# A planner's allowance for transfers: two microseconds on every landing, and queries loaded right behind keys and values

## The chip, the cores and the metric

The kernel runs on one core of one Trainium2 chip. The metric is the device time of one execution in microseconds (us); of the kernel before there are 8 timed executions, and one further look with the hardware profiler.

## The reference, cut to what matters

Linear attention with cosine weights feeds a two-layer network with squared ReLU. Eight batches (B), eight heads (H), 576 positions (S), head width 64 (D); the network goes from 512 to 2048 and back.

```python
def phi(x, c, s):
    r = np.maximum(x, 0.0)
    return np.concatenate([r * c, r * s], axis=-1)
q_p = phi(q, cos_w, sin_w)
k_p = phi(k, cos_w, sin_w)
kv = np.einsum('bhsf,bhsd->bhfd', k_p, v)
z = np.sum(k_p, axis=2)
num = np.einsum('bhsf,bhfd->bhsd', q_p, kv)
den = np.einsum('bhsf,bhf->bhs', q_p, z)[..., None] + 1e-06
x = (num / den).transpose(0, 2, 1, 3).reshape(B * S, H * D)
h = x @ w_in
out = np.maximum(h, 0.0) ** 2 @ w_out
```

## The kernel before, in words

The work goes batch by batch, as a pipeline. The 576 positions of a batch are four tiles of 128 (j = 0 to 3) and a tail of 64 (j = 4, tiles whose names end in t). For each batch b there are:

- loads of k, v and q from HBM, each one transfer of 1 MB (`load_main`, L325) and two tail transfers of 64 KB (`load_tail`, L334). There is one buffer each for k, v and q, so that a batch's load waits for the last reader of the batch before it;
- features (`declare_feature`, L470): ReLU times cosine or sine, from k into kp and from q into qp, on ScalarE (ACT) or VectorE (DVE), and the cast of v into vx (`declare_v`, L483);
- kz (`declare_kz`, L493): the products of kp and vx on TensorE (PE), five steps j that gather in two PSUM banks, the tail last;
- transposes of qp by DMA (`declare_qT`, L530) on the queue of SyncE (SP); for batches 0 and 1 by TensorE instead (`declare_qT_pe`, L543);
- num (`declare_num`, L565): the five numerator products on PE, each followed on DVE by `div`, three instructions that divide into x; then transposes of x by DMA (`declare_xT`, L610), again on SP;
- the first layer: plain products for batches 0 to 2 (`declare_plain`, L665), and from batch 3 on a scheme with seven products in place of eight (`declare_seven1`, L763: P1 to P7, with copies of partial sums by ACT at L793, L797 and L800, ReLU by ACT, `rs` by DVE). Tails of several batches go together (`declare_tails`, L699);
- the second layer: plain rows at first (`declare_rows`, L943), then again seven products (`declare_pair`, L869: Q1 to Q7, with sums `gs` on DVE and copies on ACT), and a store of the rows from `ysb` on GpSimd's queue (POOL).

The attention of batch b + 2 is spread among the two layers of the batches b and b + 1. No engine's order is written by hand. Every step is declared with `add` (L58): which engines may do it and for how long, what it reads and writes, and for PE steps a place `pos` on a common time line; T1[b] and T2[b] (L419) are the places at which the layers of batch b begin. `Planner.plan` (L110) then builds all orders at once: at each step it takes, over all engines, the operation that can start first, and between those that can start at the same time the one with the smaller due time `late` (or, on PE, `pos`). PE may run ahead of its places by no more than 4.5 us (`window`). The instructions are issued in exactly that order, and each engine works through its own list in order.

When the planner takes a step to be done decides what it puts behind it. For a transfer (`size` given) that is L182: the transfers share one pipe, each begins 2.2 us after its issue at the earliest (`land`), and takes `size`: 3.4 for 1 MB of k, v or q, 0.4 for a tail, 2.6 for a quarter of the weights, 1.7 for a store, 0.9 or 0.4 for a DMA transpose. A DMA transpose also holds SP's queue in the plan until 2.0 us before it is done (`held`).

Loads of batch b + 2 are declared in the loop at the end (L1165 on): k and v on SP after the last transpose of qp of batch b + 1 is issued, q on SP after the last transpose of x of batch b + 1 is issued. kz of batch b + 2 is placed at T2[b] + 5.5, its five num from T1[b + 1] + 0.3 on at a distance of 1.75.

Of the kernel before, what the change touches and what calls it, by code (L numbers as in the profile page):

```python
# [19 lines left out]
class Buf:  # L20


    def __init__(self, pool):
        self.pool, self.i, self.users = pool, None, 0
# [10 lines left out]
class Planner:  # L35
# [7 lines left out]

    HOP = 0.07

    def __init__(self, pools, window, in_turn):
        self.in_turn = in_turn
        self.free = {p: [(0.0, i) for i in range(n)] for p, n in pools.items()}
        self.window = window
        self.ops, self.writer, self.readers = [], {}, {}  # L50
        self.turns = {}
# [6 lines left out]
    def add(self, engs, fn, r=(), w=(), pos=None, lat=None, size=None, after=(), land=2.2, held=None):  # L58
        if isinstance(engs, tuple):
            engs = {engs[0]: engs[1]}  # L60
        if size:
            lat = land + size
        op = Op(engs, fn, pos, lat, size)
        op.land, op.held = land, held
        for k in r:
            if k in self.writer:
                op.deps.add(self.writer[k])
            self.readers.setdefault(k, []).append(op)
        for k in w:
            if k in self.writer:  # L70
                op.deps.add(self.writer[k])
            op.deps.update(x for x in self.readers.get(k, ()) if x is not op)
            self.writer[k], self.readers[k] = op, []
        for k in list(r) + list(w):
            b = k[0] if isinstance(k, tuple) else k
            if isinstance(b, Buf) and b not in op.bufs:
                op.bufs.append(b)
                b.users += 1
        op.after = set(after) - op.deps
        op.deps |= op.after  # L80
        self.ops.append(op)
        return op
# [27 lines left out]
    def plan(self, t0):  # L110
        ops = self.ops
        for n, op in enumerate(ops):
            op.n = n
            for d in op.deps:
                d.succ.append(op)
        pe = sorted((o for o in ops if "PE" in o.engs), key=lambda o: (o.pos, o.n))
        t = t0["PE"]
        for o in pe:
            o.late = o.slot = t
            t += o.engs["PE"]  # L120
        for o in reversed(ops):
            d = max(o.engs.values()) + (o.lat or 0.16)
            for s in o.succ:
                o.late = min(o.late, s.late - d)
            if "PE" not in o.engs:
                ends = [
                    s.slot + s.engs["PE"]
                    for s in o.deps
                    if "PE" in s.engs and any(b in s.bufs for b in o.bufs if b.pool in "FB")
                ]  # L130
                if ends:
                    o.late = min(o.late, max(ends) + 1.0)
        clock = dict(t0)
        waiting = {o: len(o.deps) for o in ops}
        pipe = 0.0
        ready = {e: [] for e in clock}
        order = []

        def arm(o):
            for e in o.engs:  # L140
                ready[e].append(o)

        for o in ops:
            if not o.deps:
                arm(o)
        left = len(ops)
        head = 0
        while left:
            best = None
            while head < len(pe) and pe[head].start is not None:  # L150
                head += 1
            for e in clock:
                cand = []
                for o in ready[e]:
                    if e == "PE" and o.slot > pe[head].slot + self.window:
                        continue
                    s = max(clock[e], o.pos if e not in ("PE",) and o.pos else 0.0)
                    for d in o.deps:
                        ordered = d in o.after or d.eng == e and e in ("PE", "ACT", "DVE")
                        s = max(s, d.end if ordered else d.done)  # L160
                    s = self.room(o, s)[0]
                    if s is not None:
                        cand.append((s, o))
                if not cand:
                    continue
                s0 = min(c[0] for c in cand)
                s, o = min(
                    (c for c in cand if c[0] <= s0 + 1e-9),
                    key=lambda c: (c[1].slot if e == "PE" else c[1].late, c[1].n),
                )  # L170
                if best is None or s < best[0]:
                    best = (s, e, o)
            if best is None:
                stuck = [o for o in pe if o.start is None][:6]
                raise RuntimeError(f"stuck: {[(o.fn.__name__, o.pos, o.n) for o in stuck]}")
            s, e, o = best
            for x in o.engs:
                ready[x].remove(o)
            o.eng, o.start, o.end = e, s, s + o.engs[e]
            o.done = o.end + (o.lat if o.lat is not None else 0.17 if e == "PE" else 0.09) + self.HOP  # L180
            if o.size:
                pipe = o.done = max(o.end + o.land, pipe) + o.size  # L182
                if o.held is not None:
                    o.end = max(o.end, o.done - o.held)
            clock[e] = o.end
            for b, i in self.room(o, s)[1]:
                b.i = i
                self.free[b.pool] = [f for f in self.free[b.pool] if f[1] != i]
            for b in o.bufs:
                b.users -= 1  # L190
                b.last = max(getattr(b, "last", 0.0), o.done)
                if b.users == 0:
                    self.free[b.pool].append((b.last, b.i))
            for x in o.succ:
                waiting[x] -= 1
                if not waiting[x]:
                    arm(x)
            order.append(o)
            left -= 1
        return order  # L200
# [3 lines left out]
def kernel(  # L204
# [82 lines left out]
    def at(buf, name=None):  # L287
        return mem[name or buf.pool][:, buf.i]
# [67 lines left out]
    def put(b, tt, y, c0=0, c1=DM, eng=None, n=1):  # L356
        dst = bass.AP(
            tensor=out.tensor,
            offset=(b * S + tt) * DM + c0,
            ap=[[J * DM, P], [1, n * DM if n > 1 else c1 - c0]],  # L360
        )
        eng.dma_start(out=dst, in_=y.rearrange("p i c -> p (i c)") if n > 1 else y[:, c0:c1])  # L362

    def put_tails(m, y):
        for i in range(2):
            dst = bass.AP(
                tensor=out.tensor,
                offset=((2 * m + i) * S + MAIN) * DM,
                ap=[[DM, TAIL], [1, DM]],
            )  # L370
            nc.gpsimd.dma_start(out=dst, in_=y[i * TAIL : (i + 1) * TAIL, :])

# [30 lines left out]


    LOAD = 3.4
    T_MM, T_MM128, T_MM65, T_TR = 0.1092, 0.0586, 0.0296, 0.066
    plan = Planner(POOLS, 4.5, ("gs1", "gs2", "gs3", "gs4"))
    add = plan.add  # L410
    PROD1, PROD2 = 4 * T_MM, 8 * T_MM

# [439 lines left out]
    def four(b):  # L852
        return 0 if b < 7 else 1
# [12 lines left out]
    def w2_keys(i, j):  # L866
        return [("w2", 2 * i + n) for n in range(2)]

    def declare_pair(b, pair, t):  # L869
        A, Bk, E = plan.buf("F"), plan.buf("B"), plan.buf("F")  # L870
        u = plan.buf("u")
# [61 lines left out]

        def store(_):
            if pair < 2:
                put(b, 2 * pair, at(y), n=2, eng=nc.gpsimd)
            else:
                for i in range(2):
                    put_tails(four(b) * 2 + i, at(y)[:, i])

        add(("POOL", 0.6), store, r=keys(0) + keys(1), size=1.7)

    def declare_rows(b, tiles, t, f_banks):  # L943

# [212 lines left out]
    for b in range(2, B):  # L1157
        if b > 2:
            if b in SEVEN:
                declare_x_sums(b)  # L1160
                for r in range(4):
                    declare_seven1(b, r, T1[b] + r * 7 * PROD1)
            for m, first, n in TAILS[b]:
                for i in range(first, first + n):
                    declare_tails(m, 2 * i, T2[b] - 1.5 + 0.01 * i)  # L1165
        if b + 2 < B:
            for nm in "kv":
                declare_load(b + 2, nm, "SP", after=[turned["q", b + 1, J // 2]])
            declare_load(b + 2, "q", "SP", after=[turned["x", b + 1, J // 2]])
            declare_att(b + 2, T2[b] + 5.5, [T1[b + 1] + 0.3 + 1.75 * j for j in range(NS)])  # L1170
        for i, pair in enumerate(PAIRS[b]):
            declare_pair(b, pair, T2[b] + i * 7 * PROD2)

# [34 lines left out]
```

## Time and profile before

| | |
|---|---|
| median of 8 timed executions | 287.98 us (287.23 to 288.65) |
| the profiled execution's own time | 288.65 us |
| its span, from the first to the last instruction | 286.9 us |
| granted TensorE clock | 0.999 |
| busy: PE, weight loads, DVE, ACT | 273.5, 225.6, 218.8, 192.2 us |
| k, v, q on SP: issue to landing, median | 7.3, 9.9, 6.8 us |

The span is what the profile shows; the profiled execution took 1.75 us more, which lie around the span. PE's busy time overstates it, since matmuls overlap in the records: how much PE loses is read from the distances between the starts of its groups. A row of the timeline reads: start, length, engine, line, operation, tiles written and read, form, count, and in brackets the engine's idle time before it and what ended it. Times in the traces count from the start of the span.

### The profile page before, as it was taken

What the parts mean: (1) busy time and instruction counts of PE and PEld (TensorE: products, weight loads), DVE (VectorE), ACT (ScalarE), POOL (GpSimd) and SP (SyncE); (2) the same over time, 40 slices, a digit from 0 to 9 for tenths busy, and PEclk for the clock granted to TensorE, in tenths of its full rate; (3) what the DMA queues carried; (4) which work ended last, traced back from release to release, by engine and by line L of the source; (5) the groups of instructions that cost most, each with busy time, mean ns of one, the idle gap of its engine ahead of it and who ended that gap; (6) DMA issues with size and microseconds to landing.
All of it is one profiled execution on the core that took longest, in us unless ns stands there. A gap on an engine that the chain in (4) does not pass through costs nothing.

```text
span 286.9 us, 7068 instructions
## 1 busy us (share of the span) xinstructions
PE 273.5 (95%) x2827; PEld 225.6 (79%) x2827; DVE 218.8 (76%) x512; ACT 192.2 (67%) x379; POOL 39.6 (14%) x67
## 2 busy tenths in 40 slices
PE   8899999999999999998997999987999999999994
PEld 3478856788588888886896888876889888888883
DVE  1668999987954987599957898779965999179651
ACT  3676844696985887769846995599735853584521
POOL 8816246100000000000010000000022000100021
PEclk9999999999999999999999999999999999999999
DMA  7999999689999949996799848997195400210015
GB/s 237 296 206 310 332 216 376 202 157 281 290 216 234 278 115 203 239 331 169 123 221 325 168 125 169 258 265 201 36 204 97 135 2 0 93 55 2 1 75 146
DMA packets 77569, 53.02 MB, mean 185 GB/s; under 512 B 52032, under 2 KB 73024, under 8 KB 77536
## 3 DMA queue, kind: packets, MB, share of 16 engines
q1 hardware_dynamic: 67856, 29.76, 46.5%
q0 software_dynamic: 9536, 22.68, 27.2%
q8 instruction: 22, 0.36, 0.5%
q10 hardware_dynamic: 144, 0.13, 0.1%
q14 instruction: 11, 0.09, 0.1%
HBM read 36.70 MB, written 9.44 MB: 161 GB/s over the span
## 4 chain that ended last, share of the span: by engine, by line
PE 58%; DVE 20%; DMA 11%; ACT 4%; SPq 3%; issue 2%; POOL 2%; POOLq 0%; DVEq 0%; ACTq 0%
PE banks L401 55%; DVE gT L390 6%; DMA kt<-in_k_dram 6%; DVE rs L393 4%; DMA k<-in_k_dram 3%; DMA q<-in_q_dram 2%; DVE gs L398 2%; DVE w1s L398 2%; SPq L329 1%; DVE qp L379 1%; ACT rt L387 1%; DVE kp L379 1%; SPq L337 1%; ACT kp L377 1%; PE banks L551 1%
## 5 line engine op out<-in xcount | busy, mean ns | idle before, releaser
L401 PEld LDWEIGHTS <-w1sb 128*128 128x128 bf16 x784 | 73.0, 98 | 10.6 <-issue 2.6
L401 PE MATMUL banks<-xT,w1sb 128*128 128x256 bf16 (+1 forms) x576 | 68.2, 267 | 0.6 <-DVE x L599 0.4
L401 PEld LDWEIGHTS <-gs 128*128 128x128 bf16 x480 | 46.5, 98 | 7.4 <-DVE gs L398 1.2
L401 PE MATMUL banks<-w2sb,gT 128*128 128x256 bf16 (+1 forms) x304 | 50.2, 306 | 0.7 <-ACT banks L905 0.5
L401 PEld LDWEIGHTS <-gT 128*128 128x128 bf16 x408 | 38.4, 98 | 13.6 <-issue 1.3
L387 ACT ACTIVATE rt<-banks 128x512 bf16<-128x512 f32 x64 | 37.6, 600 | 13.5 <-PE banks L401 8.9
L401 PEld LDWEIGHTS <-w1s 128*128 128x128 bf16 x320 | 30.6, 98 | 8.4 <-issue 4.7
L362 POOL DMA_DIRECT2D out_dram<-ysb x15 | 8.1, 541 | 209.1 <-DVE ysb L398 83.7
L393 DVE CUSTOM_DVE_ANT_0 rs<-banks,sums 128x512 bf16<-128x512 f32 x40 | 27.2, 684 | 5.6 <-ACT sums L800 4.8
L401 PE MATMUL banks<-w2sb,gs 128*128 128x256 bf16 x240 | 30.9, 273 | 0.4 <-DVE ysb L398 0.4
L401 PE MATMUL banks<-w2s,gs 128*128 128x256 bf16 x240 | 30.0, 273 | 0.5 <-DVE gs L398 0.3
L390 DVE TENSOR_TENSOR gT<-rt 128x512 bf16<-128x512 bf16 x48 | 19.9, 421 | 12.8 <-ACT rt L387 12.3
L390 DVE TENSOR_TENSOR gT<-rs 128x1024 bf16<-128x1024 bf16 (+1 forms) x50 | 28.2, 579 | 1.6 <-ACT rs L387 0.8
L398 DVE TENSOR_TENSOR ysb<-banks,sums 128x256 f32<-128x256 f32 x30 | 12.6, 421 | 20.0 <-ACT sums L914 9.5
L401 PE MATMUL banks<-xs,w1s 128*128 128x256 bf16 x160 | 23.7, 273 | 2.1 <-ACT banks L793 2.1
L387 ACT ACTIVATE rs<-banks 128x512 bf16<-128x512 f32 x40 | 23.4, 608 | 2.0 <-PE banks L401 2.0
L401 PE MATMUL banks<-xT,w1s 128*128 128x256 bf16 x160 | 22.3, 272 | 1.6 <-DVE rs L393 1.5
L377 ACT ACTIVATE qp<-q,sin_col 128x512 bf16<-128x512 f32 x32 | 22.7, 730 | 1.3 <-DMA q<-in_q_dram 1.3
L377 ACT ACTIVATE kp<-k,sin_col 128x512 bf16<-128x512 f32 x32 | 22.6, 734 | 0.7 <-DMA k<-in_k_dram 0.7
L599 DVE TENSOR_TENSOR x<-banks,den 128x512 bf16<-128x512 f32 x30 | 20.7, 691 | 1.0
L398 DVE TENSOR_TENSOR gs<-gT 128x1024 bf16<-128x1024 bf16 x26 | 17.9, 688 | 1.7 <-PE banks L401 1.1
L401 PE MATMUL banks<-xTt,w1sb 128*128 128x256 bf16 x128 | 15.6, 273 | 0.0
(106 smaller groups left out, 373.3 us busy)
## 6 DMA issues: line engine op xcount, KB each, us to landing
out_dram<-ysb POOLq DMA_DIRECT2D x15, 512.0 KB, 4.2
k<-in_k_dram SPq DMA_DIRECT2D x6, 1024.0 KB, 7.3
v<-in_v_dram SPq DMA_DIRECT2D x5, 1024.0 KB, 9.9
q<-in_q_dram SPq DMA_DIRECT2D x5, 1024.0 KB, 6.8
v<-in_v_dram POOLq DMA_DIRECT2D x3, 1024.0 KB, 9.9
w1sb<-in_moe_w_in_dram POOLq DMA_DIRECT2D x4, 512.0 KB, 11.1
w2sb<-in_moe_w_out_dram POOLq DMA_DIRECT2D x4, 512.0 KB, 12.3
q<-in_q_dram POOLq DMA_DIRECT2D x2, 1024.0 KB, 9.3
```

The lines of the kernel that those rows point to most:

```text
L329: eng.dma_start(out=main[:, :, js, :], in_=src[b, :, 0:MAIN, :].rearrange("h (p j) d -> p h j d", j=J)[:, :, js, :],)
L337: eng.dma_start(out=tail[g * TAIL : (g + 1) * TAIL, :, :], in_=src[b, g * HH : (g + 1) * HH, MAIN:S, :].rearrange("h p d -> p h d"),)
L362: eng.dma_start(out=dst, in_=y.rearrange("p i c -> p (i c)") if n > 1 else y[:, c0:c1])
L377: nc.scalar.activation(out=dst, in_=src, func=ACTF.Relu, scale=col)
L379: nc.vector.tensor_scalar(out=dst, in0=src, scalar1=0.0, scalar2=col, op0=ALU.max, op1=ALU.mult)
L387: nc.scalar.activation(out=out, in_=in_, func=ACTF.Relu)
L390: nc.vector.tensor_tensor(out=out, in0=in_, in1=in_, op=ALU.mult)
L393: nc.vector._custom_dve(TENSOR_ADD_SAT, out=out, in0=in0, in1=in1, s0=float("inf"), s1=0.0)
L398: nc.vector.tensor_tensor(out=out, in0=in0, in1=in1, op=op)
L401: nc.tensor.matmul(out=out, lhsT=lhsT, rhs=rhs, start=start, stop=stop, skip_group_check=True)
L551: nc.tensor.transpose(t[:, h, :], qp_at(b, j)[:, h, :], ident[:, :])
L599: nc.vector.tensor_tensor(out=x_at(b, j).rearrange("p (b k) (l d) -> p b k l d", b=n, l=2), in0=n4[:, :, :, 0:D].rearrange("p b (k l) d -> ...
```

## The change

The planner gets a `margin`, here 2.0 us: a transfer counts as done for whoever reads it, or wants its buffer, 2 us after its end in the pipe; the pipe itself and the hold of SP's queue go on as they were. The margin holds for every step with a `size`: loads of k, v, q and of the weights, DMA transposes, stores. In the loop, q is declared right behind k and v, with the same condition. kz of batch b + 2 is placed at T1[b + 1] - 7.5, which is T2[b] + 5.9 for most batches and T2[5] + 12.0 for batch 7; num begins at T1[b + 1] - 2.0 in place of + 0.3. The remaining lines let stores go to SP from batch 99 on, which no batch reaches: all stores stay on POOL.

```diff
-    def __init__(self, pools, window, in_turn):
+    def __init__(self, pools, window, in_turn, margin):
+        self.margin = margin
...
             if o.size:
-                pipe = o.done = max(o.end + o.land, pipe) + o.size
+                pipe = max(o.end + o.land, pipe) + o.size
+                o.done = pipe + self.margin
                 if o.held is not None:
-                    o.end = max(o.end, o.done - o.held)
+                    o.end = max(o.end, pipe - o.held)
...
+    LATER = -2.0
...
-    plan = Planner(POOLS, 4.5, ("gs1", "gs2", "gs3", "gs4"))
+    plan = Planner(POOLS, 4.5, ("gs1", "gs2", "gs3", "gs4"), 2.0)
...
+    def st_name(b):
+        return "SP" if b >= 99 else "POOL"
...
+    def st_eng(b):
+        return nc.sync if b >= 99 else nc.gpsimd
...
         if b + 2 < B:
-            for nm in "kv":
+            for nm in "kvq":
                 declare_load(b + 2, nm, "SP", after=[turned["q", b + 1, J // 2]])
-            declare_load(b + 2, "q", "SP", after=[turned["x", b + 1, J // 2]])
-            declare_att(b + 2, T2[b] + 5.5, [T1[b + 1] + 0.3 + 1.75 * j for j in range(NS)])
+            declare_att(b + 2, T1[b + 1] - 7.5, [T1[b + 1] + LATER + 1.75 * j for j in range(NS)])
```

The instructions are the same in kind and number on PE (2827 matmuls), ACT and DVE, but for a few features that the planner gives to ACT instead of DVE or the reverse, and groups of several calls that stand together; what changes is their order, on all engines.

More of the change, by code (lines that the diff above doesn't have):

```diff
@@ L362, in put, with put_tails @@
         eng.dma_start(out=dst, in_=y.rearrange("p i c -> p (i c)") if n > 1 else y[:, c0:c1])
-    def put_tails(m, y):
+    def put_tails(m, y, eng):
         for i in range(2):
@@ L370, in put_tails @@
             )
-            nc.gpsimd.dma_start(out=dst, in_=y[i * TAIL : (i + 1) * TAIL, :])
+            eng.dma_start(out=dst, in_=y[i * TAIL : (i + 1) * TAIL, :])
     def relu_scale(eng, dst, src, col):
@@ L935, in store @@
             if pair < 2:
-                put(b, 2 * pair, at(y), n=2, eng=nc.gpsimd)
+                put(b, 2 * pair, at(y), n=2, eng=st_eng(b))
             else:
                 for i in range(2):
-                    put_tails(four(b) * 2 + i, at(y)[:, i])
-        add(("POOL", 0.6), store, r=keys(0) + keys(1), size=1.7)
+                    put_tails(four(b) * 2 + i, at(y)[:, i], st_eng(b))
+        add((st_name(b), 0.6), store, r=keys(0) + keys(1), size=1.7)
     def declare_rows(b, tiles, t, f_banks):
```

## The prediction, as it was made before the run

> **What bounds the kernel now.** I read the page first. Busy shares say that PE is the bound, and that DVE and ACT are too full to forgive much:
>
> ```profile
> PE 273.5 (95%) x2827; PEld 225.6 (79%) x2827; DVE 218.8 (76%) x512; ACT 192.2 (67%) x379; POOL 39.6 (14%) x67
> ```
>
> No matmul is added or removed, so the question is how long PE stands still, and on whom. Second, the waits of all engines, longest first (us in total, times, longest). Those on transfers of k and kt, and PE's own:
>
> ```profile
> ACT kp L377 <- DMA k<-in_k_dram: 5.6, 5, 2.1
> ...
> PE banks L401 <- ACT banks L793: 2.1, 2, 1.4
> ...
> DVE kpt L379 <- DMA kt<-in_k_dram: 2.0, 2, 1.1
> ...
> PE banks L401 <- DVE rs L393: 1.5, 2, 0.9
> ...
> PE banks L401 <- DVE vx L384: 1.2, 2, 1.0
> ```
>
> PE hardly waits for a transfer itself in the steady part; it waits for ACT and DVE, and these have waited for k. The timeline near 155 us (the load of batch 6) shows how:
>
> ```profile
> 154.31 0.61 PE L401 MATMUL banks<-xs,w1s 128*128 128x256 bf16 x4
> ...
> 155.07 0.72 ACT L377 ACTIVATE kp<-k,cos_col 128x512 bf16<-128x512 f32 x1 [2.06 <-DMA k<-in_k_dram]
> ...
> 155.70 0.58 ACT L793 COPY banks<-banks 128x512 f32<-128x512 f32 x1
> ...
> 156.33 0.60 PE L401 MATMUL banks<-xs,w1s 128*128 128x256 bf16 x4 [1.41 <-ACT banks L793]
> ```
>
> ACT stands 2.06 us before a feature that nobody needs yet; the copy that PE needs is queued behind it. A 256-wide matmul starts every 109 ns (four in 0.43 us at 153.09 to 153.52), so from 154.31 to 156.33 PE lost 2.02 - 4 x 0.109 = 1.58. I cost each stall so, start to start. The timeline near 191 us (batch 7) has the same with kt on DVE, and the last two lines the head of the chain that follows:
>
> ```profile
> 191.71 0.35 DVE L379 TENSOR_SCALAR kpt<-kt,cos_col 128x256 bf16<-128x256 f32 x1 [1.08 <-DMA kt<-in_k_dram]
> ...
> 194.64 1.03 PE L401 MATMUL banks<-xT,w1s 128*128 128x256 bf16 x8
> ...
> 196.45 0.60 PE L401 MATMUL banks<-xs,w1sb 128*128 128x256 bf16 x4 [0.78 <-ACT sums L800]
> ...
> 197.95 0.60 PE L401 MATMUL banks<-xT,w1s 128*128 128x256 bf16 x4 [0.90 <-DVE rs L393]
> ```
>
> **What the Trainium skill says.** "Perfetto Trace Analysis", Sequencer Loop: an engine's instruction waits for its semaphores in that engine's queue, so what stands behind it waits too; the 2.06 us agree. "DMA: Bandwidth & Descriptors", Issuing engines are not separate DMA queues: transfers of all issuers interleave on the same 16 DMA engines. The trace agrees: where k, v and q of batch 3 go out in a row from 65.39, they land at 71.24, 74.00 and 77.86, one behind the other. Same page, Rules for kernel authors: issue a DMA early and wait for it late; the margin is a way to wait later. "TensorE: Matmul & The Clock Gate", Back-to-back issue gap: its isolated formula gives 256 / 2.4 + 2.5 = 109 ns, which the trace shows; the lower spacing that it states for streams of weight load and matmul is not seen here.
>
> **The change part by part.**
>
> *Margin on loads.* Features stand later in the lists of ACT and DVE, relative to PE's products. The order of the changed kernel shows it where it counts: for batches 6 and 7 the first feature of k on ACT comes behind the copy "banks<-banks 128x512" (L793) which it now precedes; for batches 6 and 7 kpt's cosine, too, goes from DVE to ACT, further back. Stalls of PE today that begin with a late k or kt:
> - (a) ACT on k: 1.58 at 156.33 and 0.69 - 0.44 = 0.25 at 157.45; 1.26 - 0.44 = 0.82 at 188.05 and 0.25 at 189.17. Sum 2.90. Bounds 1.5 to 2.9 regained; I take 2.6, since the copy comes first.
> - (b) after kt on DVE: 0.23 at 194.64, 1.81 - 8 x 0.109 = 0.94 at 196.45, 1.50 - 0.44 = 1.06 at 197.95. Sum 2.23. ACT is full there as well (5.00 of 5 us busy from 195 to 200), so I take half, 1.1; bounds 0 and 2.2.
> - (c) batch 4: ACT waits 0.87 for k at 95.50, then does five kp and three vx almost in a row; PE loses 0.56, 0.28 and 0.22 at 99.49, 101.73 and 102.82, 1.06 in all. Half, 0.5; bounds 0 and 1.1.
>
> *num 2.3 us earlier.* Four `div` of 1.06 us (0.16 + 0.20 + 0.69, rows at 94.85 on) and one of 0.75 leave DVE's crowded end of the first layer. There, from 122.96 to 135.95, the chain that ended last runs through DVE without a pause, and PE loses 0.75, 0.29 and 0.50 at 133.40, 135.27 and 135.99: 1.54. But q's features may come in earlier. Half, 0.8; bounds -0.5 and 1.5. num itself waits for qpT; in batch 4 it starts within 0.04 us of the landings at 117.55 and 119.79, so it can't come earlier there unless the transposes do; the planner's margin on transposes keeps PE from standing before them.
>
> *q behind v.* No bytes are added. q's issue (about 0.6 us of SP, as its two tails each) passes, on SP, those of kt and vt and the transposes of x. Today v lands at 159.32 and kt at 159.52; with q between (batch 3) v landed at 74.00 and kt at 78.04. kt, vt and the first transpose of x come up to 3.8 us later. Cover: ACT's kpt sine came 6.1 to 9.0 us after kt's landing in batches 4 to 7 (168.65 against 159.70, for one), and kz's tail step 7.9 us and more. Nothing in the forecast; the second rival is this cover gone.
>
> *Margin on weights, at the head.* The planner counts the first quarter of w_in as landed 2 us later, and puts the 16 transposes of qp ahead of the first 24 plain products. Today:
>
> ```profile
> 18.51 1.33 ACT L377 ACTIVATE qp<-q,sin_col 128x512 bf16<-128x512 f32 x2
> 18.66 1.05 PE L401 MATMUL banks<-xT,w1sb 128*128 128x128 bf16 x16 [0.23 <-ACT xT L384]
> ...
> 19.55 1.06 PE L551 MATMUL banks<-ident,qp 128*128 128x128 bf16 x16
> ...
> 20.45 2.36 PE L401 MATMUL banks<-xT,w1sb 128*128 128x128 bf16 x24
> ```
>
> The first quarter of w_in had landed at 16.62. PE now does 24 products, 16 transposes and 8 more by 20.45 + 8 x 0.056 = 20.90. With the new order it waits for ACT's sine features, which end at 19.18 and 19.84: 8 transposes to 19.65, 8 from 19.88 to 20.33, then 32 products x 0.056 = 1.79, to 22.12. That is 1.2 later, and PE is never idle long from here to 42.5, where it waits 0.2 for vx: 1.0 lost. Bounds 0.6 and 1.3.
>
> *New waits.* All lists are reshuffled while DVE and ACT keep their 218.8 and 192.2 us of work; margins on stores keep `ysb` longer in the plan. The trace can't show these; I bound them by 0 and half of what is regained, and take a quarter: 1.2.
>
> Sum: 2.6 + 1.1 + 0.5 + 0.8 = 5.0 regained, 1.0 + 1.2 = 2.2 lost, net 2.8 us. Against the profiled execution: 288.65 - 2.8 = 285.85, span 286.9 - 2.8 = 284.1. That execution was 0.67 above the median; for the median 287.98 - 2.8 = 285.2. On POOL, k and q of batch 2 are swapped (k first). I cost that at nothing, since the lists of ACT and DVE have batch 2's kp ahead of its qp now; uncovered it would be 2.6 us of DVE (50.47 - 47.84).
>
> **The rivals.**
>
> 1. *The stalls only move.* ACT and DVE are the scarce thing; features put later crowd the second layer. For it: 4.9 of 5 us busy on DVE from 160 to 175. Against it: the waits on k are pure idling of ACT, 2.06 and 1.30 us. Half of (a) regained, nothing else, and the lost terms 1.0 and 0.5: 288.0.
> 2. *Slower: kt behind q.* The features of kt stand in in-order lists, and if kt lands later than planned, ACT or DVE stands before it as it does before k today, with PE's copies behind. The planner takes kt as landed 0.7 + 2.2 + 3 x 3.4 + 0.4 + 2.0 = 15.5 us after k's issue. Today kt needs 10.6 to 12.7 (191.42 - 178.77), with q ahead 14.4 to 16.5 by the above. It decides from 15.5 on. Price: 1 us over, at (b)'s rate of 2.2 us of PE for 1.08 us of standing, about 2 us in each of two batches: 285.2 + 4 = 289.2.
> 3. *All is regained.* (a) to (c) and the 1.54: 7.7, no new waits, 1.0 lost: 281.3. Against it: DVE's fullness.
>
> That the change does nothing is excluded by the orders.
>
> **How the numbers follow.** Forecast 0.63 (its own range 283.2 to 287.2), rival 1 0.13, rival 2 0.14, rival 3 0.10. The range reaches from inside rival 3 to inside rival 2, 282.6 to 288.6, leaving about 1 in 10 on each side. Within 0.2% (about what a measurement can tell from no change) is 287.4 to 288.6: most of rival 1 and edges, 0.11; slower, rival 2 with a few of rival 1: 0.15; faster 0.74.
>
> **What would show it.** Right: the idle time before kp on k falls from 5.6 to about 2 or less, the idle 1.41 and 0.65 of PE behind L793 are gone, PE's transposes of qp start near 19.2 with an idle time of about 1 us before them. Wrong: waits of ACT or DVE on kt above 2 us in total (rival 2), or PE's idle times behind `rs`, `gs` and `x` as long as before (rival 1).

## The result, and the profile after

The changed kernel took 285.29 us (median of 11, 284.5 to 286.45), the kernel before in the same comparison 288.17 (median of 32). The ratio is 0.9904, with a 95% interval of 0.988 to 0.9927: 2.8 us were gained (2.1 to 3.5), where 2.8 had been forecast. The profiled execution after took 284.12, its span 282.3, at a clock of 1.0. One remark for the numbers below: the kernel before, places_alone, kp_later_by_hand, all_later_by_hand (13 of 22 times), margin_1 and no_margin_on_weights fall now and then into executions 3 to 5 us longer, which ratios leave out and medians don't, and the profiled executions of four of them (places_alone, kp_later_by_hand, all_later_by_hand, margin_1) were of that kind, so that of these the order is read, and the lengths of waits only beside each other's.

The page first. PE's busy time fell by 2.5 us with the same matmuls, and DVE and ACT were busy as long as before to within 1.2 us:

```profile
PE 271.0 (96%) x2827; PEld 226.3 (80%) x2827; DVE 217.6 (77%) x512; ACT 191.8 (68%) x379; POOL 39.6 (14%) x67
```

The waits of ACT alone, in the changed kernel (us in total, times, longest). Those on k were 5.6 us, 0.7 of them on the first load; the 0.2 left is the first load alone. No row of kt is left on either engine, and DVE's 4.7 us on k (5.2 before) is the first load too, before anything can run:

```profile
ACT vx L386 <- DMA v<-in_v_dram: 1.1, 3, 0.6
...
ACT kp L379 <- DMA k<-in_k_dram: 0.2, 1, 0.2
```

The timeline of the changed kernel at the load of batch 6. k landed at 152.25 and the first feature of it starts at 153.03, behind both copies of L796, which were L793; PE waits here only for qpT's tail:

```profile
148.86 0.59 ACT L796 COPY banks<-banks 128x512 f32<-128x512 f32 x1
...
150.53 0.32 PE L403 MATMUL banks<-kvz,qpTt 128*64 128x65 bf16 x8 [0.21 <-DMA qpTt<-qpt]
...
152.54 0.57 ACT L796 COPY banks<-banks 128x512 f32<-128x512 f32 x1
...
153.03 0.73 ACT L379 ACTIVATE kp<-k,cos_col 128x512 bf16<-128x512 f32 x1
```

At batch 7, the place of (b): the copy that PE waits for stands behind a cast of v now, and kt is read at 195.67, 4.6 us after the 191.1 at which it landed:

```profile
191.63 0.62 ACT L386 CAST vx<-v 128x512 bf16<-128x512 f32 x1
...
192.14 0.59 ACT L803 COPY sums<-banks 128x512 f32<-128x512 f32 x1
...
192.79 0.60 PE L403 MATMUL banks<-xs,w1sb 128*128 128x256 bf16 x4 [0.81 <-ACT sums L803]
...
195.67 0.52 ACT L379 ACTIVATE kpt<-kt,cos_col 128x256 bf16<-128x256 f32 x1
```

The head, where the loss was forecast: the transposes of qp stand ahead of all 32 plain products, and PE waits for ACT's sine:

```profile
16.98 1.33 ACT L379 ACTIVATE qp<-q,sin_col 128x512 bf16<-128x512 f32 x2
17.76 1.23 PE L554 MATMUL banks<-ident,qp 128*128 128x128 bf16 x16 [1.30 <-ACT qp L379]
...
18.83 1.95 PE L403 MATMUL banks<-xT,w1sb 128*128 128x128 bf16 x32
```

To see the whole, I sum what PE lost: for each matmul, the distance to the start of the next less the undisturbed spacing of its form (109 ns for 256 columns, 216, 56 and 29 for 512, 128 and 65; in the two forms of the tails, 64x65 and 128*64, every second matmul starts 3 to 4 ns after the one before it, and 4 and 3 are taken for all, which adds the same 3.3 us to the total of either kernel). Three parts: the start (up to the second group of transposes of x, L1107, at 17.59 before and 16.07 after), the head (to the first product of the second layer), and the rest.

| kernel | start | head | rest |
|---|---|---|---|
| before | 5.43 | 0.97 | 16.75 |
| after | 3.91 | 2.22 | 12.47 |

The two starts run the same instructions; after's loads came 1.5 us sooner in this execution, which no order explains. So of the 4.5 us between the two profiled executions 3.0 are put down to the change: 4.3 regained in the rest, 1.25 lost at the head.

### The profile page after: what moved, and what is told of

Its sections match the earlier page's. It is cut to its first block, busy times and chain, and to the rows that moved or that the text cites. A ratio compares the mean times of both kernels' runs of the same rounds, so it can differ in the third digit from the quotient of the medians.

```text
span 282.3 us, 7076 instructions
## 1 busy us (share of the span) xinstructions
PE 271.0 (96%) x2827; PEld 226.3 (80%) x2827; DVE 217.6 (77%) x512; ACT 191.8 (68%) x379; POOL 39.6 (14%) x67
## 4 chain that ended last, share of the span: by engine, by line
PE 75%; DVE 13%; DMA 5%; ACT 3%; issue 2%; SPq 1%; ACTq 0%; DVEq 0%
PE banks L403 69%; DMA q<-in_q_dram 5%; DVE gT L392 4%; PE banks L1041 3%; DVE gs L400 3%; DVE rs L395 2%; PE banks L554 1%; ACT rs L389 1%; DVE kp L381 1%; DVE x L602 1%; SPq L331 1%; PE banks L642 1%; PE banks L1104 1%; DVE xs L400 0%; PE banks L1079 0%
## 5 line engine op out<-in xcount | busy, mean ns | idle before, releaser
L403 PE MATMUL banks<-xs,w1s 128*128 128x256 bf16 x160 | 23.0, 272 | 0.0
## 6 DMA issues: line engine op xcount, KB each, us to landing
q<-in_q_dram SPq DMA_DIRECT2D x5, 1024.0 KB, 13.5
```

Of the source, the lines that this page charges most:

```text
L403: nc.tensor.matmul(out=out, lhsT=lhsT, rhs=rhs, start=start, stop=stop, skip_group_check=True)
```

## The experiments

The theory after the result: in-order lists on ACT and DVE stood before late transfers, with PE's copies behind; the margin moved the features back and with that freed the copies. The rivals: one of the three places (q, num, kz) pays, and the margin is beside the point; or the plan as a whole came out luckier, and no part has a worth of its own. All ratios are to the kernel before.

**The two halves.** margin_alone is the changed kernel with q, kz and num placed as before; places_alone is the changed kernel with margin 0.0.

```diff
-    LATER = -2.0
+    LATER = 0.3
...
-            for nm in "kvq":
+            for nm in "kv":
...
+            declare_load(b + 2, "q", "SP", after=[turned["x", b + 1, J // 2]])
-            declare_att(b + 2, T1[b + 1] - 7.5, ...
+            declare_att(b + 2, T2[b] + 5.5, ...
```

> The changed kernel with q, kz and num declared where the kernel before has them; the margin of 2 us stays. Theory 1 (the margin is what regains the stalls, by keeping late features out of the way): the greater part of the gain stays, 285 to 287 us, and ACT's waits on k fall to under 2 us. Theory 2 (q and num declared earlier pay for the margin; without them the planner must hold num and the first layer back for transposes that it counts 2 us late, and these holds are in the order): slower than the kernel before, 289 us or more, although ACT hardly waits for k.

> The changed kernel with a margin of 0: q behind v, kz and num at the new places. Theory 1: ACT stands on k as before, 5 us in all, and at least two thirds of the gain is lost: 287 to 288.5 us; the head is as in the kernel before (no idle time of 1.3 us ahead of the transposes of qp). Theory 2: the places alone give the gain, and the head's loss of 1.2 us goes too: 284 to 286 us.

margin_alone: 1.0058 (1.0036 to 1.008). places_alone: 1.0125 (1.0065 to 1.0185). Each half alone is slower than before, places_alone more so than either theory had it; together they gain 1%. In places_alone k is late all over. The order suggests why: what follows it was moved forward, and nothing allows for its landing. ACT stands 2.7 us before k of batch 4 and 3.6 before k of batch 5, where kp_later_by_hand below, in the order of before up to there, has 1.8 and none. The waits of ACT in places_alone:

```profile
ACT kp L379 <- DMA k<-in_k_dram: 8.5, 5, 3.6
```

In margin_alone the waits on k are gone as in the changed kernel (0.5 us in all on ACT), and yet PE loses 3.7 us between 130 and 140 us, against 1.2 in the changed kernel. The timeline of margin_alone shows one such place: the features and casts were put later, and now it is they, not their transfers, that stand ahead of PE's copy.

```profile
131.32 1.13 ACT L386 CAST vx<-v 128x512 bf16<-128x512 f32 x2
...
132.35 0.58 ACT L800 COPY sums<-banks 128x512 f32<-128x512 f32 x1
...
132.99 0.60 PE L403 MATMUL banks<-xT,w1s 128*128 128x256 bf16 x4 [1.00 <-ACT sums L800]
```

So a wait that is gone is not yet time that is gained. The second theory had the time right, but not the place: PE stood before DMA transposes for 0.4 us in all.

**The three places, one at a time** put back, the margin kept.

```diff
-            for nm in "kvq":
+            for nm in "kv":
...
+            declare_load(b + 2, "q", "SP", after=[turned["x", b + 1, J // 2]])
```

> The changed kernel, but q of batch b + 2 is declared as before, behind the last transpose of x of batch b + 1; margin 2.0, kz at T1 - 7.5 and num at T1 - 2.0 stay. Theory 1 (the early q is what lets the margin pay: with a late q the chain q, qp, transpose, num, div pays two margins one after the other and holds PE): about as slow as the margin alone, ratio to before 1.000 to 1.008, with PE losing over 3 us behind qpT, num and the sums after it in batches 3 to 7. Theory 2 (the early kz and num are what pays; q's place is a detail): 0.988 to 0.993, as the changed kernel.

```diff
-    LATER = -2.0
+    LATER = 0.3
```

> The changed kernel, but num at T1 + 0.3 as before; margin 2.0, early q and kz stay. Theory 1 (early q is what lets the margin pay, and num 2.3 us earlier is worth the 0.8 us that the prediction gave it in batch 5): 0.992 to 0.995. Theory 2 (num's place decides, since div must be away from DVE's crowded end of the first layer in every batch): 0.998 to 1.006. If num's place is worth nothing: 0.988 to 0.992.

```diff
-            declare_att(b + 2, T1[b + 1] - 7.5, ...
+            declare_att(b + 2, T2[b] + 5.5, ...
```

> The changed kernel, but kz of batch b + 2 at T2[b] + 5.5 as before; margin 2.0, early q and early num stay. The order differs from the changed kernel's in the stage of batch 7 alone. Theory 1 (q and num are what lets the margin pay, each nearly in place of the other; kz's place is a detail): as the changed kernel, ratio to before 0.988 to 0.993. Theory 2 (both kernels that lack one of q and num still gained 0.6%, so it is kz, which all three of them have, that turns the loss of the margin alone into a gain): 0.996 to 1.006, with PE losing over 2 us more than the changed kernel between 185 and 205.

q_late: 0.9941 (0.9918 to 0.9964). num_as_before: 0.9935 (0.9907 to 0.9963). kz_as_before: 0.9869 (0.9819 to 0.9918). kz's place is worth nothing that can be seen. q is worth 0.4%, about 1 us (median 286.36); the first theory on q_late, that nothing is left without the early q, fell. num is worth 0.3% by its ratio and rather more by its median, 287.80, on the same chip as q_late: 1 to 2.5 us. Both intervals overlap with that of the changed kernel, so neither place alone is clear of the noise by its ratio. The profiles point the same way: PE's loss in the rest is 15.53 in q_late and 16.01 in num_as_before against 12.47, and of either difference about 1.1 is no loss, since five records of 512-wide matmuls are missing from each of the two traces. With both back, and kz, it is margin_alone: 17.75 and a ratio of 1.0058, over 1% worse than with either one alone put back.

**Work moved by hand.** In a plan that is built anew nothing stays in its place, so three kernels take an order as it is and move only the suspects. kp_later_by_hand: the kernel before, for batches 6 and 7 three features of k each behind two more of ACT's other steps.

```diff
-        for op in plan.plan(t0):
+        order = plan.plan(t0)
+        for tag in [("k", b, j, c) for b in (6, 7) for j, c in ((1, "c"), (0, "s"), (0, "c"))]:
...
+            order.remove(kp)
+            order.insert(order.index(copies[1]) + 1, kp)
+        for op in order:
```

> The kernel before with six instructions moved by hand: of the batches 6 and 7, the first three features of k on ACT come two of ACT's copies later; nothing else is moved, no load is earlier. Theory 1 (ACT's list stands before a late k with PE's copies behind it): most of the 2.9 us that PE loses at 156, 157, 188 and 189 us is regained, 1.5 to 2.9 us, so 285.3 to 286.7. Rival (stalls only move, since ACT is full): less than 0.7 us is regained, the same time of PE is lost a few us later.

0.9982 (0.9954 to 1.001): 0.5 us, at most 1.3, and not clear of no change, where 1.5 and more were expected. The wait on k before that copy is gone, and the next late transfers have its place. The timeline of kp_later_by_hand:

```profile
164.16 0.62 ACT L384 CAST vx<-v 128x512 bf16<-128x512 f32 x1 [0.94 <-DMA v<-in_v_dram]
164.58 0.35 DVE L379 TENSOR_SCALAR kpt<-kt,cos_col 128x256 bf16<-128x256 f32 x1 [2.40 <-DMA kt<-in_k_dram]
164.69 0.58 ACT L794 COPY banks<-banks 128x512 f32<-128x512 f32 x1
...
165.32 0.60 PE L401 MATMUL banks<-xs,w1s 128*128 128x256 bf16 x4 [1.55 <-ACT banks L794]
```

So the cast of v and the features of kt went back too. all_later_by_hand: the kernel before, for batches 6 and 7 the first three features of k and the first cast of v behind three more of ACT's steps, the cosines of k's third and fourth tile and of kt behind three more of DVE's.

```diff
+        for b in (6, 7):
+            for eng, tags, n in (("ACT", (("k", 0, "c"), ("k", 0, "s"), ("k", 1, "c"), ("v", 0, "c")), 3), ("DVE", (("k", 2, "c"), ("k", 3, "c"), ("k", 4, "c")), 3)):
...
+                    order.remove(o)
+                    order.insert(order.index(others[n - 1]) + 1, o)
```

> Planner and places of before (no margin). Of its order only this is changed, for batches 6 and 7: on ACT the first cosine and sine of k, the second cosine of k and the first cast of v each stand three other ACT steps later; on DVE the cosines of k's third and fourth tile and of kt stand three other DVE steps later. Theory 1 (the loss of before in these two stages, 2.90 us behind k on ACT and 2.23 behind kt on DVE, is in-order lists standing before k, then v, then kt; moving k alone only uncovered v and kt): 1.5 to 3.5 us of PE regained, a ratio of 0.988 to 0.995, and the waits of ACT on k and v and of DVE on kt in batches 6 and 7 fall under 1 us in sum. Theory 2 (ACT and DVE are full there, so work put later by hand crowds what follows, and only a new plan as a whole gains): under 0.7 us, 0.9975 to 1.005, with the waits on transfers gone all the same.

0.9932 (0.989 to 0.9973): 2.0 us regained (0.8 to 3.2), within what the first theory gave, by two batches alone and with nothing else changed. The medians of the executions that the ratio counts, 287.28 against 288.24, give 1.0 us only, which lies between the two theories. So the mechanism pays, and that is the cleanest test of it here, but between 1 and 2 us the size is open. ACT and DVE stand before no k, v or kt of batches 6 and 7 any longer, as both theories had it (the 3.0 us that DVE stands before a kt, at 102.67, are batch 4, where nothing was moved). And some of the stalls move: from 150 to 215 us PE waits 2.9 us in all (4.5 over the same work in kp_later_by_hand), and what is left stands mostly behind ACT's other copies. PE's waits in all_later_by_hand from 150 to 215:

```profile
PE banks L401 <- ACT sums L802: 1.3, 2, 0.9
...
PE banks L401 <- ACT banks L795: 0.5, 1, 0.5
```

head_back: the changed kernel, with three plain products (24 matmuls) put ahead of the transposes of qp.

```diff
-        for op in plan.plan(t0):
+        order = plan.plan(t0)
+        first = next(i for i, o in enumerate(order) if o.fn.__name__ == "tr")
+        early = [o for o in order if o.fn.__name__ == "plain"][:3]
+        order = order[:first] + early + [o for o in order[first:] if o not in early]
+        for op in order:
```

> The changed kernel with three products (24 matmuls of 128 columns) of the first layer moved back ahead of the transposes of qp, in the order of instructions alone; all else is as the planner has it. If the head's loss is as predicted, 1.2 us (1.46 lost there now against 0.39), the time falls by 0.7 to 1.2 us against the changed kernel, to about 284.3; if DVE's chain from the first divisions to vx sets the time there, by less than 0.3 us.

284.45 us (282.59 to 285.12), 0.9846 (0.9801 to 0.9892). The timeline of head_back has PE's products where before had them; the idle 1.30 is gone:

```profile
18.46 1.05 PE L403 MATMUL banks<-xT,w1sb 128*128 128x128 bf16 x16 [0.23 <-ACT xT L386]
19.35 1.06 PE L554 MATMUL banks<-ident,qp 128*128 128x128 bf16 x16
...
20.24 0.61 PE L403 MATMUL banks<-xT,w1sb 128*128 128x128 bf16 x8
```

PE's loss is 1.71 at its head against 2.22, and 12.30 in the rest against 12.47. By the profile 0.7 us were won, by the middles of the ratios 1.7; the intervals of this kernel and of the changed one overlap a little, so the size is open. By its median it is the fastest kernel of this study, with kz_as_before (284.55) hardly behind.

**Which transfers need the margin.** margin_on_loads gives it to the loads of k, v and q alone, no_margin_on_weights to all but the quarters of w_in.

```diff
-                o.done = pipe + self.margin
+                o.done = pipe + (self.margin if o.fn.__name__ == "load" else 0.0)
```

> The changed kernel, with the margin of 2.0 only on the loads of k, v and q; weights, DMA transposes and stores count as done at their end in the pipe as before. Theory 1 (the gain is features put behind late k, v and kt; the margin on weights costs about 1 us at the head): 283 to 285 where the changed kernel takes 285.3, ratio to before 0.982 to 0.989, with PE's loss at the head gone. Theory 2 (transposes need the margin as much as the loads do, since qpT came late in the kernel with the places alone): PE waits for qpT and x again, over 2 us in sum, and the ratio is 0.993 to 1.005.

```diff
-                o.done = pipe + self.margin
+                o.done = pipe + (self.margin if o.eng != "GIVEN" else 0.0)
```

> The changed kernel, with the margin on all transfers but the quarters of w_in, which count as done at their end in the pipe. Its order has 24 plain products ahead of the transposes of qp at the head again. With the kernel that has the margin on the loads of k, v and q alone it differs in the margin on DMA transposes and w_out. Theory 1 (weights' margin costs 1 us at the head and transposes need it): 283.5 to 285, ratio 0.982 to 0.989, PE waiting under 1 us for qpT and x in all. Theory 2 (the plan is so sensitive that any shift at the head reshuffles all that follows, and the gain of the version with products moved by hand doesn't carry over): 0.990 to 0.998, with the head's 1.2 us won and lost again after 80 us.

margin_on_loads: 0.998 (0.9952 to 1.0008). no_margin_on_weights: 1.0004 (0.9971 to 1.0037). Both have the head of before back, 0.97 us, and both lose it many times over in the rest: 18.32 (about 1.1 of it again five missing records) and 17.64 against 12.47. Of that about 2 us lie in one place, the same in both, which neither before nor after has: ACT wants a buffer of `ysb` whose store POOL issued at 206.50, and which landed at 215.85 only. The same store took 6.0 us in the kernel before and 5.1 in the changed one, here 9.35. A DMA transpose of qp, issued on SP at 205.80, was as slow: 10.4 us, against 7.1 and 5.1. Both were under way when POOL issued four tail stores from 211.52 on; that these slowed them is not shown. The timeline of no_margin_on_weights:

```profile
206.50 0.53 POOL L364 DMA_DIRECT2D out_dram<-ysb  x1 [23.94 <-issue]
...
215.93 0.37 ACT L916 COPY ysb<-banks 128x256 f32<-128x256 f32 x1 [3.88 <-DMA out_dram<-ysb]
...
216.35 0.37 PE L403 MATMUL banks<-kvz,qpT 128*128 128x65 bf16 x7 [1.82 <-ACT ysb L916]
```

The stores have the margin in this kernel. A change of 2 us in when w_in counts as landed, at 15 us, is all that sets no_margin_on_weights apart, and it ends in a stall at 215. These two runs don't say, then, what the margin on transposes is worth: with no_margin_on_weights as bad, margin_on_loads is no evidence for it.

**The dose.** The changed kernel with a margin of 1.0, and with one of 4.0.

```diff
-    plan = Planner(POOLS, 4.5, ("gs1", "gs2", "gs3", "gs4"), 2.0)
+    plan = Planner(POOLS, 4.5, ("gs1", "gs2", "gs3", "gs4"), 1.0)
```

> The changed kernel with a margin of 1.0 in place of 2.0. Its order has plain products ahead of the transposes of qp at the head again. Theory 1 (the margin must cover how late loads land: k came 2.06 and 1.30 us late, kt up to 1.08, and landings move by a us or more between executions): one us leaves k late by about 1 us in batches 6 and 7, so 1 to 2 us are lost there against 1.2 won back at the head: ratio 0.988 to 0.996 and waits of ACT or DVE on k, v or kt of 1.5 us and more in the steady part. Theory 2 (any margin that puts features behind PE's copies is enough): the head is won and nothing lost, 0.984 to 0.988.

> The changed kernel with a margin of 4.0. The head is as in the changed kernel. Theory 1 (at 2.0 no wait on k is left, so more care covers nothing and only lengthens the series q, qp, transpose, num, div, x by 2 us at each transfer): slower than the changed kernel by 1 to 4 us, ratio to before 0.994 to 1.004. Theory 2 (care is cheap, the planner finds other work to fill): within 0.3% of the changed kernel, 0.988 to 0.993.

With margins of 0.0, 1.0, 2.0 and 4.0, the places being those of the changed kernel, the ratios are 1.0125, 0.9944 (0.9917 to 0.9971), 0.9904 and 1.0135 (1.01 to 1.017). The interval of 1.0 overlaps with that of 2.0, so that one us is too little isn't clear of the noise; in its profile ACT stands 2.3 us before k of batch 4, in places_alone 2.7. At 2.0 and at 4.0 the only wait of ACT on k is the first load, 0.2 and 0.3 us. Two us more spare no further wait on k, and they cost some 6.6 us against the changed kernel, more than the 1 to 4 expected. Of margin_4's loss 4.71 us are at the head and 18.51 in the rest. At the head its new order even has a late load again: features of q's tail stand on DVE (and ACT) ahead of copies that PE needs, and PE loses 1.97 us there. The timeline of margin_4:

```profile
25.72 0.49 DVE L381 TENSOR_SCALAR qpt<-qt,cos_col 128x256 bf16<-128x256 f32 x1 [2.46 <-DMA qt<-in_q_dram]
...
27.26 0.94 PE L403 MATMUL banks<-xT,w1sb 128*128 128x256 bf16 x7 [1.80 <-DVE xT L386]
```

## Why the prediction was right, point by point

The signs named beforehand came: ACT's wait on k is down to 0.2 us, PE waits no more behind the copy of L793, and the transposes of qp wait 1.30 us for ACT (at 17.76, in an execution whose start was 1.5 us sooner). Of the signs of being wrong, no wait on kt is left, and PE's wait behind `rs` fell from 1.5 to 0.4 us.

PE's loss by stages, before and after, with times of the spans (the same work lies up to 4 us earlier after):

| term of the sum | stage | before | after | regained | forecast |
|---|---|---|---|---|---|
| (a) | 148 to 158 and 180 to 190 | 3.61 | 1.00 | 2.6 | 2.6 |
| (b) | 190 to 210 | 2.71 | 1.98 | 0.7 | 1.1 |
| (c) | 80 to 110 | 2.03 | 2.32 | -0.3 | 0.5 |
| (d), num earlier | 110 to 140 | 2.64 | 1.60 | 1.0 | 0.8 |
| head | to 35 | 0.97 | 2.22 | -1.25 | -1.0 |
| new waits | 158 to 180 | 1.35 | 1.68 | -0.3 | -1.2 |

What is not listed (35 to 80, 140 to 148, 210 to the end) gave back some 0.5. That the sum is so near the forecast is in part luck: (b) and (c) gave 1.2 less than forecast and the head lost 0.25 more, and against that the new waits cost 0.9 less and the unlisted stages gave 0.5.

- **(a)** held in size and in place. But its reasoning, "since the copy comes first", was too narrow: kp_later_by_hand put k behind the copy and regained about 0.5 us, because v and kt are as late; all_later_by_hand, with all three put back, regained 1 to 2. The margin covers all three, and it does so without the places: margin_alone loses 0.95 and 0.38 us in the two stretches.
- **(b)** held, in the lower half of its bounds. The wait on kt is gone, and the copies stand behind casts of v instead. ACT's fullness, for which half was taken, agrees with the row at 191.63.
- **(c)** was wrong. That the wait for k cost PE 1.06 us there was a mistake: ACT doesn't wait for k any longer (landed 95.78, first feature 97.44), and the loss stays. Already before, PE's wait at 99.49, the first and largest of the three, was ended by DVE's `x` and not by ACT. In the changed kernel it is the features themselves, five kp and a cast in a row, that stand ahead of the two ReLU steps PE needs. The timeline of the changed kernel:

```profile
99.89 0.71 ACT L379 ACTIVATE kp<-k,sin_col 128x512 bf16<-128x512 f32 x1
...
100.50 0.61 ACT L386 CAST vx<-v 128x512 bf16<-128x512 f32 x1
...
101.01 1.08 ACT L389 ACTIVATE rt<-banks 128x512 bf16<-128x512 f32 x2
...
101.65 0.32 PE L403 MATMUL banks<-kvz,qpTt 128*64 128x65 bf16 x8 [1.10 <-ACT rt L389]
```

  The row of "almost in a row" had been read and put down to the wait ahead of it.
- **(d)** held: 1.0 for 0.8. With num put back the stage loses 2.49 us again, and the wait behind `rs` at its end is there again, which the changed kernel doesn't have. The kernel before and num_as_before:

```profile
133.40 0.60 PE L401 MATMUL banks<-xT,w1s 128*128 128x256 bf16 x4 [0.59 <-DVE rs L393]
```

```profile
133.53 0.60 PE L403 MATMUL banks<-xT,w1s 128*128 128x256 bf16 x4 [0.65 <-DVE rs L395]
```

  With q put back instead, the stage loses 3.04: by these profiles num's place pays there only with the early q.
- **The head** held: 1.25 lost for 1.0, with the transposes waiting 1.30 us. That the margin on weights is the cause is shown by no_margin_on_weights, whose head is that of before to 0.01 us.
- **New waits** came, at `rs` and `gs` of batch 6, about 1.3 us in two rows of the changed kernel's timeline, and were half outweighed by a wait on `ysb` at 174.56 (0.56) that went:

```profile
162.71 0.60 PE L403 MATMUL banks<-xT,w1s 128*128 128x256 bf16 x4 [0.41 <-DVE rs L395]
...
165.44 0.83 PE L403 MATMUL banks<-w2s,gs 128*128 128x256 bf16 x6 [0.52 <-DVE gs L400]
```

- **Rival 1**, that the stalls only move, is what margin_alone does. The prediction gave it 288.0 for the whole change; it holds for half of it.
- **Rival 2**, kt behind q: kt did land 14.4 to 16.5 us after k's issue in batches 4 to 7, the range that was worked out, and so at times beyond the 15.5 that the planner counts on. It cost nothing, because kt's features came far enough back (165.31 for a landing at 160.6, 195.67 for 191.1).

What the prediction did not see is that the parts don't add. Its sum has a term for the margin and a term for the places, each positive (4.2 and 0.8), while on the chip either alone is slower than before, by 0.6% and 1.25%. Apart from the luck named above, the total came out right because the terms were read from stalls of the kernel before, stage by stage, and the change with both its halves removes those. Why the halves fail alone is seen only at the places shown, and why the plan without the margin on weights comes out 5 us worse in the rest is open beyond the 2 us of the store; both would need the plan followed step by step. That a planned order depends on such a detail also means that the 1% lies within the spread of neighbouring plans (0.987 to 1.0135 here), and is a property of this plan more than of the idea.

The prediction put v, q and k of batch 3, landing one behind the other, down as agreeing with what is said of transfers of several issuers; all three were issued by SP, so these landings don't test it.

## What to carry to other kernels

When an in-order engine stands before a late transfer, look at what is queued behind it and at all transfers that are late at that place: moving the first one alone only uncovers the next. Where a planner builds the order, an allowance for landing paid here only together with earlier loads and places, and its size can be read from the waits in the trace (the longest on k was 2.06 us; with two us of margin no wait on k was left but the first load's, and four cost 2.3% more than two). A plan built again without one part says little of that part's worth; take the order as it is and move the suspects by hand. Read a row of work before a stall twice: it may be the work itself, and not the wait at its front, that is late.

## What was not expected of the hardware

The start varies by itself. Up to the second transposes of x the kernels run the same instructions, yet PE's loss there was 3.8 to 5.9 us in the profiled executions: the first v, issued at 2.67 and 2.66 us, landed at 11.17 in before and at 9.58 after. Two single profiles differ by 1.5 us in 290 for that reason alone. And the loads took longer or shorter with what went out beside them: q, moved right behind k and v, landed 13.5 us after its issue in the median (6.8 before), v 11.0 (9.9), k 6.7 (7.3).
